# Feed-forward steps in three token phases of 12, 18 and 6 steps, with 30 of 36 steps in seven products

## The chip, the cores and the metric

One core of one Trainium2 chip runs the whole program. The metric is device time in microseconds (us): the median over three runs of the kernel before is 1127.13 us (1123.15 to 1127.32). The engines have short names in the profile: PE is TensorE (matmuls), PEld its weight loads, DVE is VectorE, ACT is ScalarE, POOL is GpSimd, SP is SyncE, which here issues nearly all DMA transfers (SPq is its queue). SBUF is the on-chip memory, PSUM the accumulators that the matmuls write.

## The reference

Both halves read the same tokens x (2048 tokens, 576 features); a gate mixes them.

```python
g = _sigmoid((x * gate_w).sum(-1, keepdims=True))
a = _A_ref(x, A_wqkv, A_wo)                  # linear attention, 32 heads of 18
y = _layernorm(x, axis=-1)                   # B: 576 -> 4608 -> 576
h = _gelu(jnp.einsum("bsd,df->bsf", y, w1) + b1)
b = jnp.einsum("bsf,fd->bsd", h, w2) + b2
return g * a + (1 - g) * b
```

All data is fp32. An fp32 matmul is made of several products of high and low parts ("fp32r" tiles): a value is split by a copy to fp32r on ACT (the high part) and a subtraction on DVE (the low part).

## The kernel before

**Stages.** Roughly the first 280 us compute the attention half and leave g times attention in DRAM (`late_acc`). The rest, which is all that the change touches, is the feed-forward half B. It is cut in two: the 2048 tokens into two super-blocks of 1024 (1 block is 2 x 512), the 4608 hidden features into 18 chunks of 256 (`NCHUNK`). One **step** is one chunk for one super-block, so there are 36 steps: steps 0 to 17 for super-block 0, steps 18 to 35 for super-block 1. Step 18 takes the chunk of step 17 again, whose weights are still in place (`HALF_TIME`, line 61).

**A step.** The *up* part multiplies the normalised tokens (tile `y`) by the chunk of w1 (tiles `wa` and `wb`) in the seven products of a Strassen-Winograd scheme (`FACTORS`, `UP_ORDER`; 7 matmuls of 512 columns each, so 49 in a step), and then GELU gives `h`. The *down* part multiplies `h` by the chunk of w2 (tile `region`) and adds the result to the accumulators (tile `accs`). It has two forms. In a **seven-product step** (`SEVEN`, line 64) there are 14 units of 6 matmuls of 288 columns: 84 matmuls. Four sums of parts of h must first be made (`make_sum`, line 1000; tile `u`), each then split, and four sums of w2 (`sum_w2`). In a **plain step** there are 8 units of 12 matmuls: 96, and no sums. Before, the seven-product steps are 1, 3, ... 15 and 17 to 34 (26 steps); plain are 0, 2, ... 16 and 35 (10 steps). The last step's units go to the output at once (`make_end`).

A down unit ends in an **eviction** (`evict`, line 1171): DVE adds PSUM to the accumulator, `accs<-ps,accs`, 12 in a seven-product step and 4 in a plain one. The other four of a plain step are seeded (`SEEDS`): ACT puts the old accumulator into PSUM first and copies the sum back. Two PSUM pairs take turns, so that a unit waits for the eviction two units before.

**Weights.** In steps 0 to 16 w1 of the next chunk is made from the input (`make_w1`, line 1025): SP loads it (8 transfers), POOL makes four sums of 384 columns (tile `fresh`), ACT and DVE split it into `wa` and `wb` (DVE: rows `wa<-fresh,wa` and `wb<-fresh,wb`), and SP stores the split parts in DRAM (`w1d`). In the second half these are only loaded back, one transfer for each of the seven factors (`load_split_w1`). w2 of a chunk is loaded and split in every step (`make_w2`; DVE rows `region<-fresh,region`).

**Tokens of super-block 1.** They are normalised, summed, split and stored to DRAM (`yd`) beside the first half (`make_y`, line 1204): DVE rows `accs<-accs` and `ystage<-...`. At the switch of super-blocks SP loads the seven parts of `y`, each as soon as the last product of step 17 that reads it is done; eight finishing operations on DVE (`make_finish`) mix the accumulators with attention and SP writes them out.

**The order of the work.** Every engine runs its instructions in the order in which the program lists them. A planner writes that order (`plan`, line 1278, and what follows): each operation has a cost in ns and a due time, and a list scheduler picks the next one for each engine. DVE has 9 `h` places, 5 `u` places and 7 `region` places to work with. Operations marked `port` (two inputs in SBUF) of DVE and POOL are kept apart in the plan; the program itself does not enforce that.

Of the kernel before, what the change touches and what calls it, by code (L numbers as in the profile page):

```python
# [60 lines left out]
LAST = 2 * NCHUNK - 1  # L61
SLOTS = 14
LAG = 3
# [8 lines left out]
FIRST_LANDS = 9000  # L72
SEEDS = ((0, 0, 0), (0, 1, 0), (1, 0, 0), (1, 1, 0))
SUM_ENGINE = {S1: "POOL", S3: "POOL", S2: "POOL", S4: "POOL"}
# [7 lines left out]

# [18 lines left out]
class InOrder:  # L101
# [5 lines left out]
    def __getattr__(self, name):  # L107
        op = getattr(self.engine, name)
        return lambda *args, **kwargs: self.tc.keep_in_program_order(op(*args, **kwargs))  # L109
# [3 lines left out]
def tile_gated_mix(ctx: ExitStack, tc: tile.TileContext, x, xm, xe, wm, we, wvm, wve, wo, um, ue, w2, b1, b2, gw, out):  # L113
# [670 lines left out]
    def chunk_of(k):  # L784
        return k if k < HALF_TIME else (k + NCHUNK - 1) % NCHUNK
# [72 lines left out]
    attn = [spare[:, n * D:(n + 1) * D] for n in range(6)] + [fresh[:, n * D:(n + 1) * D] for n in range(2)]  # L858
# [6 lines left out]
    class Op:  # L865

        def __init__(self, engine, f, ns, tail, needs, gives, port, take, give, by):
            self.engine, self.f, self.ns, self.tail = engine, f, ns, tail
            self.needs, self.gives, self.port = list(dict.fromkeys(needs)), gives, port
            self.take, self.give, self.by = take, give, by  # L870
            self.ready = 0.0

    ops, waiting, known, makers = [], {}, {}, {}
    rooms = {"h": [(0, n) for n in range(H_BUFS)], "u": [(0, n) for n in range(U_BUFS)],
             "w2": [(0, n) for n in range(W2_BUFS)]}
    lines = {name: [] for name in rooms}

    def op(engine, f, cols=0, needs=(), gives=(), port=False, take=None, give=(), ns=None, tail=None, more=0, by=None,
           early=0):
# [4 lines left out]
        o = Op(engine, f, ns, tail, needs, gives, port, take, give, by)  # L884
        o.early = early
# [7 lines left out]

    places = {}
    us = lambda key: u_places[:, places["u", key][0]]
    h_of = lambda key: h_places[:, places["h", key][0]]
    w2_key = lambda k, m: (k - (k == HALF_TIME), m)
    w2_of = lambda key: region[:, places["w2", w2_key(*key)][0]]
# [27 lines left out]
    def w1_key(k, a):  # L926
        return [("w1", k - (k == HALF_TIME), a)] if k else []
# [20 lines left out]
    def make_up(k):  # L948
        X, Yb, Z = [next(ff_banks) for _ in range(3)]
        free = lambda b: bank_users[b]  # L950
        y_in = lambda n: [("y", k // NCHUNK, FACTORS[n][1])] if k % NCHUNK == 0 else []
# [48 lines left out]
    def make_sum(k, m):  # L1000
# [4 lines left out]
        engine = SUM_ENGINE[m]  # L1005
# [16 lines left out]
    def dma(f, needs, gives, ns, service, early=0):  # L1022
        op(DMA, f, needs=needs, gives=gives, ns=ns, tail=service, early=early)
# [38 lines left out]
    def make_w2(k):  # L1062
        if k == HALF_TIME:
            return
# [449 lines left out]
```

## Time and profile before

| what | value |
|---|---|
| median of three runs | 1127.13 us |
| the profiled execution | 1125.78 us |
| its span (first to last instruction) | 1124.1 us |
| time outside the span | 1.7 us |
| granted TensorE clock | 1.00 |
| first up matmul of step 0 | 279.6 us from the span's start |

A "windows" view gives for each stretch of the span how long each engine was busy and, in brackets, how many instructions it had. A "lines" view groups instructions by line, engine and tiles and gives the mean duration of one, then the idle time of its engine just before. Nearly all instructions are recorded by one helper line (109), so the tiles name the work: `accs<-ps,accs` reads ps (PSUM) and accs and writes accs. A "waits" view says which engine waited for whom.

### The profile page before, as it was taken

To read this page: it belongs to the slowest core of one execution; us is meant where nothing else is said; L and a number is where in the kernel's file an instruction comes from. 1 tells how busy PE (TensorE), PEld (TensorE's weight loads), DVE (VectorE), ACT (ScalarE), POOL (GpSimd) and SP (SyncE) were. 2 spreads that over 40 slices of the span, in tenths; PEclk is the share of its full clock that TensorE was granted. 3 is DMA by queue.
4 is the path that set the end of the run, shared out by engine and by line. 5 is a ranking of instruction groups with operands and counts; after the bars stand their busy time and mean duration, and the time that the engine had idled before them with its cause. 6 is when DMAs were issued, how large, how long until landed. Compare 5 with 4: busy or idle time off the path is not lost.

```text
span 1124.1 us, 18584 instructions
## 1 busy us (share of the span) xinstructions
PE 1108.0 (99%) x6766; PEld 1003.5 (89%) x6766; DVE 888.7 (79%) x1369; ACT 642.6 (57%) x1153; POOL 385.9 (34%) x325
## 2 busy tenths in 40 slices
PE   9999999999999999999999999999999999999998
PEld 8999889999889888898988888888888888888888
DVE  4567685896787889979979997877887778778888
ACT  6667565453556665666756666345554555455542
POOL 2111112342334252634515453315433443344430
PEclk9999999999999999999999999999999999999999
DMA  6269853554636546473564549764445444444432
GB/s 177 64 88 286 168 171 141 225 204 160 210 122 213 187 162 213 150 267 126 186 221 154 197 166 373 280 234 129 120 123 147 127 115 127 138 127 124 120 109 85
DMA packets 109086, 189.42 MB, mean 169 GB/s; under 512 B 8892, under 2 KB 69068, under 8 KB 104898
## 3 DMA queue, kind: packets, MB, share of 16 engines
q1 hardware_dynamic: 108114, 187.49, 52.7%
q8 instruction: 53, 0.87, 0.3%
q10 hardware_dynamic: 720, 0.74, 0.2%
q14 instruction: 39, 0.32, 0.1%
q0 software_dynamic: 160, 0.01, 0.1%
HBM read 121.40 MB, written 66.80 MB: 167 GB/s over the span
## 4 chain that ended last, share of the span: by engine, by line
PE 72%; DVE 14%; ACT 4%; DMA 4%; issue 3%; POOL 2%; SPq 1%; ACTq 0%; DVEq 0%; POOLq 0%
PE ps L109 72%; DVE accs L109 3%; DVE h L109 3%; DMA fresh<-in_w 2%; DVE region L109 2%; SPq L109 1%; DVE wa L109 1%; POOL u L109 1%; DVE wb L109 1%; DVE den L109 1%; ACT h L109 1%; ACT u L109 1%; POOL fresh L109 1%; DVE u L109 1%; DMA w1d<-wb 0%
## 5 line engine op out<-in xcount | busy, mean ns | idle before, releaser
L109 PEld LDWEIGHTS ps<-region,h 128*128 128x128 f32 x3144 | 453.7, 188 | 45.9 <-DVE accs L109 10.0
L109 PE MATMUL ps<-region,h 128*128 128x288 f32 x3144 | 480.9, 296 | 4.0 <-DVE accs L109 2.0
L109 DVE TENSOR_TENSOR accs<-ps,accs 128x576 f32<-128x576 f32 x336 | 250.3, 752 | 89.8 <-PE ps L109 87.0
L109 POOL TENSOR_TENSOR fresh<-fresh 128x288 f32<-128x288 f32 (+1 forms) x164 | 173.8, 1066 | 406.2 <-DMA fresh<-in_w 332.0
L109 PE MATMUL ps<-y,wa 128*128 128x512 f32 x1008 | 269.7, 393 | 1.4 <-ACT ps L109 1.1
L109 PE MATMUL ps<-y,wb 128*128 128x512 f32 x756 | 204.3, 396 | 1.2 <-ACT u L109 1.0
L109 PEld LDWEIGHTS ps<-y,wa 128*128 128x128 f32 x1008 | 176.3, 188 | 27.2 <-DVE wa L109 1.7
L109 DVE TENSOR_TENSOR h<-u,h 128x512 fp32r<-128x512 f32 x222 | 177.1, 811 | 7.2 <-ACT u L109 4.3
L109 POOL TENSOR_TENSOR u<-u 128x512 f32<-128x512 f32 x104 | 152.3, 1465 | 88.1 <-DVE h L109 46.8
L109 PEld LDWEIGHTS ps<-y,wb 128*128 128x128 f32 x756 | 132.5, 188 | 24.7 <-ACT u L109 1.6
L109 PE MATMUL ps<-y 128*128 128x288 f32 (+1 forms) x896 | 126.9, 297 | 3.6 <-DVE acc L109 2.2
L109 ACT ACTIVATE u<-ps 128x512 f32<-128x512 f32 x73 | 43.7, 598 | 151.4 <-PE ps L109 151.4
L109 PEld LDWEIGHTS ps<-y 128*128 128x128 f32 x896 | 122.3, 188 | 7.0 <-DVE acc L109 3.4
L109 DVE TENSOR_TENSOR region<-fresh,region 128x576 fp32r<-128x576 f32 x120 | 107.8, 898 | 2.4 <-ACT region L109 1.9
L109 ACT ACTIVATE region<-fresh 128x576 fp32r<-128x576 f32 x120 | 73.9, 628 | 33.9 <-PE ps L109 33.9
L109 ACT ACTIVATE h<-ps,b1s 128x512 fp32r<-128x512 f32 x45 | 30.9, 687 | 81.9 <-PE ps L109 81.8
L109 ACT ACTIVATE h<-u,b1s 128x512 fp32r<-128x512 f32 x73 | 52.6, 721 | 32.7 <-DVE u L109 32.7
L109 ACT ACTIVATE h<-u 128x512 fp32r<-128x512 f32 x104 | 60.2, 622 | 12.4 <-POOL u L109 12.2
L109 PE MATMUL ps<-wp,qt 128*128 128x288 f32 x448 | 63.6, 298 | 1.2 <-DVE qt L109 1.2
L109 DVE TENSOR_TENSOR u<-ps,u 128x512 f32<-128x512 f32 x73 | 50.2, 688 | 15.7 <-ACT u L109 12.1
L109 DVE TENSOR_TENSOR wa<-fresh,wa 128x512 fp32r<-128x512 f32 x64 | 50.6, 791 | 14.8 <-ACT wa L109 13.9
L109 PEld LDWEIGHTS ps<-wp,qt 128*128 128x128 f32 x448 | 60.0, 188 | 1.7 <-DVE qt L109 1.7
(122 smaller groups left out, 994.9 us busy)
## 6 DMA issues: line engine op xcount, KB each, us to landing
w1d<-wa SPq DMA_DIRECT2D x17, 1280.0 KB
wa<-w1d SPq DMA_DIRECT2D x68, 320.0 KB
fresh<-in_w SPq DMA_DIRECT2D x70, 288.0 KB
y<-yd SPq DMA_DIRECT2D x14, 1280.0 KB
w1d<-wb SPq DMA_DIRECT2D x17, 960.0 KB
wb<-w1d SPq DMA_DIRECT2D x51, 320.0 KB
yd<-ystage SPq DMA_DIRECT2D x28, 320.0 KB
fresh<-in_um SPq DMA_DIRECT2D x64, 128.0 KB
```

The lines of the kernel that those rows point to most:

```text
L109: return lambda *args, **kwargs: self.tc.keep_in_program_order(op(*args, **kwargs))
```

## The change

1. **Three phases.** Steps 0 to 11 are chunks 0 to 11 for super-block 0; steps 12 to 29 all 18 chunks for super-block 1; steps 30 to 35 the last six chunks for super-block 0 again. At step 12 the accumulators of super-block 0 are mixed with attention and stored in `late_acc` (partial results); at step 30 super-block 1 is finished and written out, and super-block 0 starts again from zero (first evictions are ACT copies); at step 32 the partial results are loaded, and the end adds to them. Tokens change twice, so y is loaded twice (7 transfers of 1280 KB each time).
2. **Seven-product steps** are 30: 1, 4, 6, 7, and 9 to 34. Plain are 0, 2, 3, 5, 8 and 35. There are five seeds in a plain step instead of four.
3. **w1 of chunks 12 to 17** is made in the middle phase (`make_prep`), piece by piece through the two staging places of `ystage` (ACT copy, two DVE subtractions, one store, 7 pieces a chunk), and loaded back in steps 24 to 29 and 31 to 35. In the first phase `make_w1` is left for chunks 1 to 11.
4. **Sums of h**: S2, S3 and S4 are made by DVE (`u<-u` on DVE) instead of POOL; S1 stays on POOL.
5. **Super-block 1's tokens** must be ready by step 12 instead of step 18. Two attention places move from `fresh` to `ystage`.
6. **The planner** is new: a `port` operation is also held back in the plan if it would be in the way of an earlier due one of the other engine, DMA is planned with issue, transfer and at most 8 under way, each kind of operation has its own offset to its due time (`TUNED`), and a POOL operation is made to wait (a semaphore) for the `port` operation of DVE that the plan has ahead of it, if that ends less than 4 us before.

```diff
-SEVEN = {*range(1, NCHUNK - 1, 2), *range(NCHUNK - 1, LAST)}
-EARLY, LATE_, SLOP, SLACK = 0, 3, 30, 300
-Y_EARLY = 10000
-SEEDS = ((0, 0, 0), (0, 1, 0), (1, 0, 0), (1, 1, 0))
-SUM_ENGINE = {S1: "POOL", S3: "POOL", S2: "POOL", S4: "POOL"}
+SPLIT=12
+SWITCH = (SPLIT, SPLIT + NCHUNK)
+STEPS = [(0, c) for c in range(SPLIT)]
+STEPS += [(1, c) for c in (SPLIT - 1, *range(SPLIT - 1), *range(SPLIT, NCHUNK))]
+STEPS += [(0, c) for c in (NCHUNK - 1, *range(SPLIT, NCHUNK - 1))]
+PREP = [14, 15, 18, 21, 18, 27]
+DVE_SUMS = set([(2, False), (2, True), (4, False), (4, True), (6, False), (6, True)])
+SEEDS = ((0, 0, 0), (0, 0, 1), (0, 1, 0), (0, 1, 1), (1, 1, 1))
...
-        engine = SUM_ENGINE[m]
+        engine = DVE if (m, k < SPLIT) in DVE_SUMS else POOL
...
-        if seeded:
+        if seeded or first and k == SWITCH[1]:
             op(ACT, lambda: copy(to, pair_ap(p)), needs=needs, gives=[key], ns=543, tail=653)
...
+    def make_prep(c):
+        at = PREP_AT(c)
+        dma(lambda: load_w1(c), raw_free["w1"] + [("p", at, 1)], [("w1raw", c)], 3200, 8)
+        for n in range(4):
+            op(POOL, lambda n=n: sum_w1(c, (n,)), 384, needs=[[("w1raw", c)], [("w1sum", c, 0)], [("w1sum", c, 1)],
+                                                              [("w1raw", c), ("w1sum", c, 0)]][n],
+               gives=[("w1sum", c, n)], port=True)
+        raw_free["w1"] = []
+        for n, a in enumerate((A11, A12, A22, S1, S2, S4, S3)):
+            at = 7 * c + n
+            to, src = y_stage[:, at % 2:at % 2 + 1], wr(c)[:, a:a + 1]
...
+            op(ACT, lambda to=to, src=src: copy(to[:, :, 0:3], src), 3 * P, needs=needs + stage_free[at % 2],
+               gives=[("phi", at)])
+            op(DVE, low, 2 * P, needs=[("phi", at)], gives=[("plo", at)], port=True)
+            op(DVE, tail, P, needs=[("phi", at)], gives=[("ptl", at)], port=True)
+            dma(store, [("plo", at), ("ptl", at)], [("w1st", c, a)], 820, early=W_EARLY)
...
+    end, sequence = plan(*TUNED)
...
+        if o.port and o.engine == DVE:
+            before = dve.last.ins.name, t
+        if o.port and o.engine == POOL and before and before[1] > s - 4000:
+            tc.add_manual_dep(pool.last.ins, before[0], mybir.DependencyInfo(
+                mybir.DependencyClass.Sync, mybir.DependencyReason.DATA), reason="order")
```

Three places show how this moves instructions. The first is DVE in a steady run of seven-product steps; `accs<-ps,accs` are evictions, `h<-u,h` low parts of h, `u<-ps,u` a sum out of PSUM, `region` rows low parts of w2. Before (second half):

```order
L109 TENSOR_TENSOR accs<-ps,accs 128x2x288 x3
L109 TENSOR_TENSOR u<-ps,u 128x512
L109 TENSOR_TENSOR h<-u,h 128x512
L109 TENSOR_TENSOR accs<-ps,accs 128x2x288 x2
L109 TENSOR_TENSOR region<-fresh,region 128x2x288
L109 TENSOR_TENSOR accs<-ps,accs 128x2x288
L109 TENSOR_TENSOR u<-ps,u 128x512
L109 TENSOR_TENSOR accs<-ps,accs 128x2x288
L109 TENSOR_TENSOR h<-u,h 128x512
```

The same engine now, in the middle phase; `ystage<-fresh,ystage` are pieces of w1 for a later chunk and `u<-u` the sums of h:

```order
L117 TENSOR_TENSOR ystage<-fresh,ystage 64x128 x2
L117 TENSOR_TENSOR accs<-ps,accs 128x2x288 x2
L117 TENSOR_TENSOR u<-ps,u 128x512
L117 TENSOR_TENSOR h<-u,h 128x512
L117 TENSOR_TENSOR ystage<-fresh,ystage 128x256
L117 TENSOR_TENSOR accs<-ps,accs 128x2x288 x2
L117 TENSOR_TENSOR h<-u,h 128x512
L117 TENSOR_TENSOR u<-u 128x512
L117 TENSOR_TENSOR accs<-ps,accs 128x2x288
L117 TENSOR_TENSOR u<-u 128x512
L117 TENSOR_TENSOR u<-ps,u 128x512
L117 TENSOR_TENSOR accs<-ps,accs 128x2x288
```

Sums and pieces of w1 now stand between the evictions. The second place is POOL in the same stretch; `fresh<-fresh` of 288 columns are sums of w2, of 384 columns sums of w1. Before:

```order
L109 TENSOR_TENSOR u<-u 128x512 x4
L109 TENSOR_TENSOR fresh<-fresh 128x288 x4
L109 TENSOR_TENSOR u<-u 128x512 x4
L109 TENSOR_TENSOR fresh<-fresh 128x288 x4
L109 TENSOR_TENSOR u<-u 128x512 x4
```

And now:

```order
L117 TENSOR_TENSOR fresh<-fresh 128x288 x5
L117 TENSOR_TENSOR u<-u 128x512
L117 TENSOR_TENSOR fresh<-fresh 128x384 x4
L117 TENSOR_TENSOR fresh<-fresh 128x288 x2
L117 TENSOR_TENSOR u<-u 128x512
L117 TENSOR_TENSOR fresh<-fresh 128x288 x6
```

A run of four sums of h in a row has become one, and sums of w1 have come in. The third place is the queue of SP ahead of step 29, the last that loads prepared weights for super-block 1; `w1d_133` is the DRAM place of chunk 17, `w1d_132` of chunk 16. In the plan before the loads at the end of its second half stood like this:

```order
L109 DMA wa<-w1d_132 128x640 x3
L109 DMA fresh<-in_w 128x2x288 x2
L109 DMA wa<-w1d_132 128x640
L109 DMA wb<-w1d_132 128x640 x3
L109 DMA fresh<-in_w 128x2x288 x2
```

Now the stores of a chunk's pieces stand between the loads, for chunk 17 its own:

```order
L117 DMA w1d_133<-ystage 128x640
L117 DMA wb<-w1d_132 128x640 x3
L117 DMA wa<-w1d_133 128x640
L117 DMA w1d_133<-ystage 128x640
L117 DMA wa<-w1d_133 128x640
L117 DMA w1d_133<-ystage 128x640 x2
L117 DMA fresh<-in_w 128x2x288 x2
L117 DMA wa<-w1d_133 128x640 x2
L117 DMA w1d_133<-ystage 128x640
L117 DMA wb<-w1d_133 128x640
```

A store waits in SP's queue for DVE, and the loads behind it wait with it.

More of the change, by code (lines that the diff above doesn't have):

```diff
@@ L784, in chunk_of @@
     def chunk_of(k):
[L785 removed]
+        return STEPS[k][1]
     def w1_of(a):
@@ L883, in op @@
             tail = ns + c
-        o = Op(engine, f, ns, tail, needs, gives, port, take, give, by)
-        o.early = early
+        o = Op(engine, f, ns, tail, needs, gives, port, take, give, by, early, issues)
         ops.append(o)
@@ L1365, in tile_gated_mix @@
[L1365 to L1377 removed]
+    ups = [o for o in ops if o.engine == PE and o.by[0] == "up"]
+    downs = [o for o in ops if o.engine == PE and o.by[0] == "down"]
+    followers = {o: [u for key in o.gives for u in users.get(key, ())] for o in ops}
@@ L1470, in tile_gated_mix, with start @@
-    while any(pending.values()):
-        picks = [(x[0], n, x[1]) for n, e in enumerate((PE, ACT, DVE, POOL, DMA)) if (x := choose(e))]
-        assert picks, {e: [(o.by, o.gives, o.needs) for o in v][:3] for e, v in pending.items()}
-        s, _, o = min(picks, key=lambda x: x[:2])
-        commit(s, o)
-    assert not any(missing[o] for o in ops), [o.gives for o in ops if missing[o]][:5]
+        def start(o):
+            s = max(free[o.engine], ready[o])
+            if o.take:
+                name, keys = o.take
+                if line[name][at[name]] is not o or len(room[name]) < len(keys):
+                    return None
+                s = max(s, sorted(t for t, _ in room[name])[len(keys) - 1])
+            if o.port:
+                s = max(s, port_until[POOL] - 135 if o.engine == DVE else port_until[DVE] + 78)
+            return s
```

411 lines of the change are left out of this document (222 added, 189 removed).

## Prediction

> **What bounds the kernel now.** I read the engine totals first, then a table of stretches, then who waits for whom.
>
> ```profile
> PE 1108.0 (99%) x6766; PEld 1003.5 (89%) x6766; DVE 888.7 (79%) x1369; ACT 642.6 (57%) x1153; POOL 385.9 (34%) x325
> ```
>
> PE is busy almost always. Its busy time counts overlapping matmuls, though, so I work with the time from one stretch's start to the next's. In the table of stretches the columns are length, then busy time (instructions) of PE, PEld, DVE, ACT and POOL, the clock, the DMA share and GB/s. The edges are starts of steps: step 0; steps 1 to 17; 18 and 19; 20 to 33; 34; 35 with the end.
>
> ```profile
> 279.60:292.00 12.40, 11.40 (x51) 9.12 (x50) 4.28 (x7) 7.73 (x13) 1.02 (x1) 1.00 0.58 186
> 292.00:695.60 403.60, 399.30 (x2359) 355.21 (x2359) 351.48 (x500) 256.97 (x419) 168.38 (x133) 1.00 0.56 192
> 695.60:742.40 46.80, 45.70 (x268) 40.35 (x268) 37.76 (x52) 21.26 (x37) 15.73 (x12) 1.00 0.75 274
> 742.40:1060.30 317.90, 317.85 (x1864) 283.69 (x1863) 249.69 (x351) 168.05 (x280) 128.34 (x112) 1.00 0.48 135
> 1060.30:1083.30 23.00, 22.89 (x135) 20.27 (x134) 18.40 (x26) 12.01 (x20) 8.84 (x8) 1.00 0.44 126
> 1083.30:1124.10 40.80, 37.40 (x243) 34.51 (x241) 34.27 (x50) 14.01 (x23) 2.60 (x2) 0.99 0.24 82
> ...
> 1107.08 13.75 PE L109 MATMUL ps<-region,h 128*128 128x288 f32 x102
> ```
>
> The last row is from the order of instructions in time: 102 down matmuls of the end without a gap. Less 0.3 us for the length of the last one, 13.45 / 101 = **0.133 us** is the price of a down matmul. Steps 20 to 33 take 317.9 / 14 = **22.7 us** each, with 49 up and 84 down matmuls, so an up matmul costs (22.7 - 84 x 0.133) / 49 = 0.235 us. At these prices the whole feed-forward part, 1764 up and 3144 down matmuls, is 415 + 418 = 833 us; 3.3 us lie between the last matmul's start (1120.8) and the end. It takes 1124.1 - 279.6 = 844.5 us. So about **8 us** are lost against the clean rate: 0.9 in step 0, 4.8 in steps 1 to 17 (833 x 0.235 + 1524 x 0.133 = 398.8 of 403.6), 1.4 in steps 18 and 19, 0.8 at the end. PE's own work is the bound; what else can be won is those 8 us.
>
> Two rows of waits for steps 1 to 17 say what the 4.8 us are:
>
> ```profile
> PEld ps L109 <- ACT ps L109: 6.8, 14, 1.1
> PEld ps L109 <- DVE accs L109: 5.1, 7, 1.1
> ```
>
> Weight loads wait for a PSUM pair that an eviction on DVE, or a copy on ACT, has not left yet. Two seven-product stretches show the cause:
>
> ```profile
> 408.90:433.40 24.50, 23.37 (x136) 20.11 (x135) 23.96 (x31) 15.30 (x25) 12.07 (x9) 1.00 0.37 128
> 505.00:528.90 23.90, 23.05 (x134) 20.16 (x133) 23.32 (x32) 15.00 (x25) 12.36 (x9) 1.00 0.36 122
> ```
>
> DVE is busy 23.96 of 24.5 us and 23.32 of 23.9, and these stretches are 1.8 and 1.2 us longer than a clean 22.7. At 249.69 / 317.9 = 79% DVE, steps 20 to 33 lose nothing.
>
> **The change, part by part.** *Four more seven-product steps.* Each has 84 down matmuls in place of 96: 4 x 12 x 0.133 = **-6.4 us**, on PE, which sets the end. If every loss went as well, the span would be 279.6 + 833 - 6.4 + 3.3 = 1109.5 us, and the time, with the 1.7 us outside the span, **1111.2 us**. The rest is how much is lost anew; call it e, today 8.
>
> *The middle phase.* A clean seven-product step has 249.69 / 14 = 17.8 us of DVE, and POOL 128.34 / 14 = 9.2. Now come three sums of h and 14 small subtractions for each of six chunks.
>
> ```profile
> L109 DVE TENSOR_TENSOR h<-u,h x222: 671/681/1776, 292.9 to 1110.5; 128x512 fp32r<-128x512 f32 x111
> L109 DVE TENSOR_TENSOR ystage<-accs,ystage x28: 410/418/426, 346.8 to 686.3; 128x256 fp32r<-128x256 f32 x28
> L109 DVE SCALAR_TENSOR_TENSOR ystage<-ystage,low_rows,accs x28: 339/345/349, 347.8 to 686.6; 128x128 fp32r<-128x128 f32 x28
> L109 POOL TENSOR_TENSOR u<-u x104: 1287/1304/1882, 310.9 to 1087.0; 128x512 f32<-128x512 f32 x104
> ```
>
> These rows give shortest, median and longest duration in ns. No sum of h has run on DVE. The nearest row is `h<-u,h`, as large and with both inputs in SBUF: 0.68 us, between 0.67 and 1.78; I take the median, since the order now keeps POOL away from it. Three make 2.0 us. A piece of w1 costs 0.42 + 0.35 us, the nearest rows for its two subtractions, so 42 pieces over 18 steps are 1.8 us a step. DVE comes to **21.6 of 22.7 us, 95%**. POOL loses three sums of 1.3 us and takes 24 sums of w1 over 18 steps; it has room and I cost that at nothing.
>
> *The first phase.* Steps 1 to 11 must carry all the work on super-block 1's tokens. Its DVE rows, and those of w1, for the first half of the feed-forward part (busy us, mean ns; behind the bar the idle time before them):
>
> ```profile
> L109 DVE TENSOR_TENSOR h<-u,h 128x512 fp32r<-128x512 f32 x94 | 82.9, 897 | 6.0 <-ACT u L109 4.3 <-ACT h L109 1.5
> L109 DVE TENSOR_TENSOR region<-fresh,region 128x576 fp32r<-128x576 f32 x43 | 44.0, 1024 | 2.3 <-ACT region L109 1.9
> L109 DVE TENSOR_TENSOR wa<-fresh,wa 128x512 fp32r<-128x512 f32 x32 | 32.6, 1019 | 13.9 <-ACT wa L109 13.9
> ...
> L109 DVE TENSOR_TENSOR wa<-fresh,wa 64x256 fp32r<-64x256 f32 x32 | 18.0, 563 | 0.9
> L109 DVE TENSOR_TENSOR accs<-accs 128x768 f32<-128x768 f32 x16 | 16.1, 1009 | 0.0
> L109 DVE TENSOR_TENSOR wb<-fresh,wb 128x768 fp32r<-128x768 f32 x16 | 15.3, 958 | 0.1
> L109 DVE TENSOR_TENSOR ystage<-accs,ystage 128x256 fp32r<-128x256 f32 x28 | 11.7, 417 | 4.0 <-ACT ystage L109 4.0
> L109 DVE SCALAR_TENSOR_TENSOR ystage<-ystage,low_rows,accs 128x128 fp32r<-128x128 f32 x28 | 9.6, 344 | 0.0
> L109 DVE TENSOR_TENSOR accs<-accs 128x384 f32<-128x384 f32 x16 | 9.2, 574 | 0.3
> L109 DVE TENSOR_TENSOR wb<-fresh,wb 64x384 fp32r<-64x384 f32 x16 | 8.9, 556 | 0.5
> ```
>
> Tokens: 16.1 + 9.2 + 11.7 + 9.6 = 46.6 us. w1: 32.6 + 18.0 + 15.3 + 8.9 = 74.8 us for 16 chunks, 4.7 each. Before, steps 1 to 17 hold about eight seven-product down parts (8 x 17.8 = 142), nine plain ones, all of that w1 and the tokens, in 351.5 us of DVE: a plain part is left with (351.5 - 142 - 74.8 - 46.6) / 9 = 9.8 us, now 9.0 (one eviction of 0.75 goes to ACT). Steps 1 to 11 of the new order carry six seven-product down parts with three sums (6 x 19.8), five plain (5 x 9.0), ten chunks (47) and the tokens: 119 + 45 + 47 + 46.6 = **258 us**. Their clean length is 11 x 22.7 + 5 x 12 x 0.133 = **258 us**. Before it was 351.5 of 398.8, 88%. So at today's durations DVE would be full.
>
> Today's durations hold time in which POOL blocks DVE: `h<-u,h` takes 897 ns here against a median of 681 in the whole run. I estimate unblocked durations of 0.75 us for `region` and 0.68 and 0.42 for the two rows of `wa`, as `h` has them for the same number of columns. Blocked are then 94 x 0.216 + 43 x 0.274 + 32 x 0.34 + 32 x 0.14 = 47 us behind 133 POOL instructions, **x = 0.36 us for each**; in steps 20 to 33 `h` runs at 736 ns and `region` at 1037, which makes 98 x 0.055 + 42 x 0.287 = 17 us behind 112, x = 0.16. These are the two rows:
>
> ```profile
> L109 DVE TENSOR_TENSOR h<-u,h 128x512 fp32r<-128x512 f32 x98 | 71.1, 736 | 0.0
> L109 DVE TENSOR_TENSOR region<-fresh,region 128x576 fp32r<-128x576 f32 x42 | 43.6, 1037 | 0.0
> ```
>
> The new order puts a POOL instruction behind a DVE one, where evictions follow, and evictions are not blocked (752 ns in steps 20 to 33, 750 in the first half). I halve x for the first phase: 70 POOL instructions x 0.18 = 12 us less, 246 of 258 us, 95%. The added wait stands on POOL; queued behind it are POOL's other sums, and ACT's copies into `region` and `h` wait for those. POOL was busy only 168 of 403.6 us here, so I cost the wait itself at nothing; it would cost a late sum if DVE ran late.
>
> How much 95% loses lies between 0 (steps 20 to 33, at 79%) and 1.5 us a step (the two stretches at 98%), over 24 seven-product steps: e between 0 and 36. I take the middle of the first phase's rows there, 0.5 us for its six seven-product steps, because tokens and w1 come in lumps, and 0.1 us for the 18 even steps of the middle: 3 + 2 us.
>
> *The switches.* Step 18 moves 396 GB/s and is still clean; step 19 loses 1.4.
>
> ```profile
> 695.60:718.30 22.70, 22.70 (x135) 20.21 (x135) 18.64 (x26) 10.38 (x19) 6.99 (x7) 1.00 1.01 396
> 718.30:742.40 24.10, 23.00 (x136) 20.14 (x135) 19.12 (x27) 10.88 (x18) 8.74 (x6) 1.00 0.51 158
> PEld ps L109 <- ACT ps L109: 2.5, 4, 1.5
> ```
>
> The wait (third row, steps 17 to 20) is for ACT, which stands behind POOL's four sums in a row; with one left, 0.4 us at each of two switches. Eight more finishing operations of DVE fall where eight evictions of step 30 go to ACT. Step 0 and the end keep their 0.9 and 0.8. The stores of w1 pieces in SP's queue cost nothing as long as a load has its 22.7 us until the next step; for chunk 17 that slack is short, at most the 14.6 us that SP has waited for a staging piece, at least nothing, and nothing is what I take:
>
> ```profile
> SPq L109 <- DVE ystage L109: 22.5, 9, 14.6
> ```
>
> The sum: e = 3 + 2 + 0.8 + 1.7 = 7.5, rounded to 7. **1111.2 + 7 = 1118.2 us**, against 1125.8 for the profiled execution, which is 1.3 us under the median of the three runs; I leave that difference alone.
>
> **Rule against row.** The long `region` rows (750 ns median, 1.0 us mean) show blocking by POOL. The Trainium skill, page "SBUF — State Buffer", section "Who interferes with whom", says that a DVE instruction with two SBUF inputs and a GpSimd instruction that reads SBUF take one shared port exclusively, and that the loser blocks fully; by that rule x could reach the whole length of a POOL instruction. That the longest `h<-u,h` took 1776 ns agrees with it; the means of 0.16 and 0.36 us do not reach it. The third rival below is what this would do here.
>
> **The rivals.** *All losses go* (e from 0 to 3): 1113 us. For it: steps 20 to 33. Against: DVE at 95% has no such stretch before. Chance 0.17. *The forecast*, e from 3 to 11: 0.45. *DVE becomes the bound in the even steps too*: 0.6 us on 24 seven-product steps, e about 17, so 1128 us, no change, and the saved matmuls are paid back in evictions. For it: 408.9 to 433.4. Against: that stretch has four POOL sums of h in a row. Chance 0.20. *POOL blocks DVE longer*: without blocking, a middle step has 21.6 - 17 / 14 = 20.4 us of DVE and 6.3 POOL instructions (5 + 24 / 18), so DVE needs more than 22.7 us once x passes 0.37 us. At x = 0.5 the middle loses 18 x 0.85 = 15 us and the first phase, 258 - 70 x 0.36 + 70 x 0.5 = 268, loses 10: e = 27 with the rest, **1138 us**, slower. For it: x was 0.36 where DVE was fullest. Against: fewer and shorter POOL instructions, and an order made for it. Chance 0.18.
>
> **How the numbers follow.** About 0.5%, 5.6 us, is what a measurement of this kernel can tell from no change. Faster by more needs e under 9: the first case and most of the second, 0.17 + 0.37 = 0.54. Within 0.5%: the rest of the second and the third, 0.28. Slower: 0.18. The range of 1111 to 1136 leaves out a few in a hundred below and about 0.15 above.
>
> **What would show it.** 48 down matmuls fewer (3096) at 0.133 us; middle steps of 22.7 to 22.9 us with DVE busy near 95%; `h<-u,h` under 750 ns in the first phase; the loss of the first phase in waits of weight loads for `accs`. The forecast is wrong if middle steps take over 23.3 us, if POOL's sums come late behind their new waits, or if a product waits for a transfer at steps 12, 29 or 30.

## The result, and the profile after

The changed kernel takes **1134.14 us** (median of 4 runs, 1133.26 to 1135.96), the kernel before 1125.89 beside it: ratio 1.0078, 95% interval 1.0053 to 1.0104. It is 0.8% slower where 0.7% faster was forecast: inside the stated range of 1111 to 1136 us, but at its slow end and on the other side of no change. The profiled execution took 1133.88 us, its span is 1132.2.

The engine totals of the changed kernel, then its table of stretches, cut at the starts of steps 0, 1, 12, 30 and 35 and at the end:

```profile
PE 1104.8 (98%) x6718; PEld 996.9 (88%) x6718; DVE 934.9 (83%) x1551; ACT 643.4 (57%) x1185; POOL 266.1 (24%) x263
```

```profile
280.00:292.10 12.10, 11.41 (x51) 9.14 (x50) 4.77 (x8) 6.51 (x11) 0.76 (x1) 1.00 0.63 212
292.10:559.90 267.80, 257.79 (x1513) 228.12 (x1512) 240.25 (x377) 173.96 (x285) 74.32 (x73) 1.00 0.63 220
559.90:977.30 417.40, 411.53 (x2397) 364.23 (x2396) 370.11 (x592) 225.06 (x399) 108.07 (x112) 1.00 0.63 195
977.30:1091.20 113.90, 113.86 (x668) 101.43 (x667) 92.51 (x138) 61.81 (x105) 21.25 (x22) 1.00 0.58 181
1091.20:1132.20 41.00, 37.44 (x242) 34.42 (x241) 34.85 (x52) 13.61 (x23) 0.00 (x0) 0.99 0.24 81
```

PE has 48 matmuls fewer (6718 for 6766). The second row holds 539 up matmuls (11 steps of 49) and, of its 1513, 974 down. At the prediction's prices, 0.235 and 0.133 us, that is 256.2 us of 267.8: 11.6 lost. The third holds 882 and 1515: 208.8 of 417.4, that is 408.8, 8.7 lost with the prices unrounded. I call these numbers **the loss** of a stretch, and work them out in the same way for every kernel, good to about 0.2 us. A plain step comes out 0.5 us below its price, so a stretch with plain steps can have a negative loss.

| loss in us | step 0 | steps 1-11 | steps 12-29 | steps 30-34 | end |
|---|---|---|---|---|---|
| before | 0.9 | 2.8 | 3.4 | 0.3 | 0.4 |
| forecast | 0.9 | 3 | 2 and 0.8 for switches | 0 | 0.8 |
| after | 0.6 | 11.6 | 8.7 | 0.3 | 0.6 |

So the matmuls were saved, and about 14 us more were lost. The losses are not spread: in the first phase step 5 alone loses 5.2 and step 4 2.7; in the middle, steps 17, 18, 19, 22 and 24 lose 2.0, 1.3, 1.1, 1.8 and 1.1, and the others little. The four steps at the two switches (12, 13, 30, 31) lose 0.3 us at most.

Who waits for whom says where to look. The rows are of the changed kernel, the first phase (first fence) and the middle (second): engine and tile, what it waited for, us in total, times, longest (`yd<-ystage` are stores of token pieces, `w1d<-ystage` of pieces of w1).

```profile
ACT wa L117 <- POOL fresh L117: 14.6, 8, 2.8
...
ACT ystage L117 <- DMA yd<-ystage: 9.3, 7, 4.2
PEld ps L117 <- ACT ps L117: 8.4, 8, 3.7
PEld ps L117 <- DVE accs L117: 7.2, 12, 1.2
```

```profile
ACT ystage L117 <- DMA w1d<-ystage: 16.5, 7, 3.0
...
PEld ps L117 <- DVE accs L117: 9.2, 20, 1.3
PEld ps L117 <- DVE region L117: 3.3, 4, 1.1
```

Besides the late evictions that were foreseen ACT now has two waits that were hardly there before: for stores of staged pieces (before, once, for 3.8 us) and, in the first phase, for POOL's sums of w1 (before, in the same steps, 0.5 us). PE in turn waits for ACT. The order in time inside step 5 shows how a wait for a store becomes a wait of PE (start, duration, what it is, and in square brackets the idle time before it):

```profile
391.82 0.35 SPq L117 DMA_DIRECT2D yd<-ystage  x1
...
396.86 0.52 ACT L117 ACTIVATE ystage<-accs 128x384 fp32r<-128x384 f32 x1 [1.99 <-DMA yd<-ystage]
397.29 0.63 ACT L117 ACTIVATE accs<-ps 128x576 f32<-128x576 f32 x1
397.82 0.67 ACT L117 ACTIVATE region<-fresh 128x576 fp32r<-128x576 f32 x1
398.40 0.62 ACT L117 ACTIVATE h<-u 128x512 fp32r<-128x512 f32 x1
398.92 0.64 ACT L117 ACTIVATE ps<-ps 128x576 f32<-128x576 f32 x1
...
399.61 1.86 PE L117 MATMUL ps<-region,h 128*128 128x288 f32 x12 [3.33 <-ACT ps L117]
```

The store is issued at 391.82, and the copy that reuses its staging place starts 5.0 us later. ACT takes its work in the listed order: the eviction of a seeded unit (`accs<-ps`), two splits (`region`, `h`) and the next seed (`ps<-ps`) stand behind that copy, and PE idles 3.33 us for the seed.

A stretch of step 19 in the middle shows the other engine. POOL makes two sums of w1:

```profile
727.05 2.45 POOL L117 TENSOR_TENSOR fresh<-fresh 128x384 f32<-128x384 f32 x2 [6.06 <-DMA wb<-w1d]
727.27 1.35 DVE L117 TENSOR_TENSOR u<-u 128x512 f32<-128x512 f32 x1
...
728.54 2.11 DVE L117 TENSOR_TENSOR h<-u,h 128x512 fp32r<-128x512 f32 x2
...
731.37 0.80 PE L117 MATMUL ps<-region,h 128*128 128x288 f32 x4 [0.82 <-DVE region L117]
```

Beside those 2.45 us of POOL, DVE's sum takes 1.35 us in place of the middle's mean of 0.71, and its two low parts 2.11 in place of 1.48 (twice 0.742); what they delay, PE waits for.

### The profile page after: what moved, and what is told of

Same layout as the page of the kernel before. It is cut to its first block, busy times and chain, and to the rows that moved or that the text cites. A ratio compares the mean times of both kernels' runs of the same rounds, so it can differ in the third digit from the quotient of the medians.

```text
span 1132.2 us, 18790 instructions
## 1 busy us (share of the span) xinstructions
PE 1104.8 (98%) x6718; PEld 996.9 (88%) x6718; DVE 934.9 (83%) x1551; ACT 643.4 (57%) x1185; POOL 266.1 (24%) x263
## 4 chain that ended last, share of the span: by engine, by line
PE 62%; DVE 20%; DMA 7%; ACT 4%; issue 3%; SPq 2%; POOL 1%; ACTq 0%; DVEq 0%; POOLq 0%
PE ps L117 62%; DVE accs L117 6%; DVE h L117 4%; DVE u L117 3%; DVE region L117 3%; SPq L117 2%; DMA yd<-ystage 2%; DVE ystage L117 1%; DMA fresh<-in_ue 1%; POOL fresh L117 1%; DVE wa L117 1%; DVE wb L117 1%; DMA w1d<-ystage 1%; ACT u L117 1%; DMA fresh<-in_um 1%
## 5 line engine op out<-in xcount | busy, mean ns | idle before, releaser
L117 PEld LDWEIGHTS ps<-region,h 128*128 128x128 f32 x3096 | 446.8, 188 | 59.3 <-DVE accs L117 18.1
L117 DVE TENSOR_TENSOR accs<-ps,accs 128x576 f32<-128x576 f32 x356 | 263.3, 751 | 34.2 <-PE ps L117 32.2
L117 POOL TENSOR_TENSOR fresh<-fresh 128x288 f32<-128x288 f32 (+1 forms) x176 | 165.9, 946 | 514.5 <-DMA fresh<-in_w 169.2
L117 DVE TENSOR_TENSOR h<-u,h 128x512 fp32r<-128x512 f32 x234 | 165.8, 732 | 12.2 <-ACT u L117 11.8
L117 DVE TENSOR_TENSOR region<-fresh,region 128x576 fp32r<-128x576 f32 x124 | 87.5, 715 | 2.0 <-ACT region L117 1.5
L117 DVE TENSOR_TENSOR u<-u 128x512 f32<-128x512 f32 x90 | 65.9, 733 | 7.8 <-POOL u L117 7.4
L117 ACT ACTIVATE h<-u 128x512 fp32r<-128x512 f32 x120 | 71.0, 618 | 2.0 <-DVE u L117 2.0
L117 ACT ACTIVATE h<-ps,b1s 128x512 fp32r<-128x512 f32 x41 | 28.1, 685 | 64.3 <-PE ps L117 64.2
L117 POOL TENSOR_TENSOR u<-u 128x512 f32<-128x512 f32 x30 | 38.8, 1294 | 101.7 <-DVE h L117 81.7
```

Source lines behind the costliest of these rows:

```text
L117: self.last = self.tc.keep_in_program_order(op(*args, **kwargs))
```

## The experiments

All ratios stand against the kernel before on the same chip. Differences in us between two kernels go across chips, on which the kernel before took 1124.5 to 1125.9 us, so they are good to about 1 us; the losses come from one profiled execution each. The kernels that leave work out keep the changed kernel's planned order, unless it says otherwise.

| kernel | us | ratio to before, 95% interval | loss in steps 1-11 | 12-29 |
|---|---|---|---|---|
| changed kernel | 1134.14 | 1.0078, 1.0053 to 1.0104 | 11.6 | 8.7 |
| no staging stores | 1125.02 | 0.9999, 0.9986 to 1.0012 | 5.6 | 6.2 |
| no subtractions of pieces | 1126.24 | 1.0017, 1.0004 to 1.0029 | 6.7 | 4.7 |
| no waits on POOL | 1150.25 | 1.0223, 1.0183 to 1.0263 | 14.3 | 19.3 |
| all sums of h on POOL | 1150.66 | 1.0232, 1.0203 to 1.026 | 29.6 | 7.8 |
| no w1 pieces | 1123.3 | 0.999, 0.998 to 1.0 | 12.2 | -2.2 |
| no sums of w1 in the middle | 1129.38 | 1.0046, 1.003 to 1.0062 | 11.5 | 3.3 |
| longer stores in the plan | 1133.13 | 1.0081, 1.0066 to 1.0096 | 12.5 | 8.2 |
| two phases, 26 seven-product steps | 1121.67 | 0.9976, 0.9965 to 0.9986 | 6.3 | -2.3 |
| two phases, 30 | 1123.26 | 0.9983, 0.9971 to 0.9996 | 7.4 | 4.0 |
| two phases, 30, tokens spread | 1133.04 | 1.0067, 1.0045 to 1.0089 | 7.5 | 12.2 |
| no tokens | 1120.1 | 0.9953, 0.9938 to 0.9969 | -3.0 | 8.2 |
| two phases, 26, sums on POOL | 1133.86 | 1.0074, 1.005 to 1.0098 | 16.8 | 0.5 |

### Which work the losses come from

**Tokens left out.** The loads, sums, splits and stores of super-block 1's tokens go; it reads those of super-block 0.

```diff
-dma(lambda j=j: load_pair(1, j), raw_free["rows"], [("yraw", j)], 2000, 7)
+dma(lambda j=j: None, raw_free["rows"], [("yraw", j)], 2000, 7)
...
-op(DVE, lambda j=j, n=n: sum_pair(1, j, n), 3 * P, port=True,
+op(DVE, lambda j=j, n=n: None, 3 * P, port=True,
```

> The changed kernel in its planned order, but the normalised tokens of super-block 1 are not made (their loads, sums, splits and stores are left out), and super-block 1 reads the tokens of super-block 0 instead. Theory A, tokens are what the first phase loses by: steps 1 to 11 lose at most 2 us (11.6 before), about 1124 us. Theory B, w1 and the three sums of h on DVE crowd it by themselves: 5 us or more stay in steps 1 to 11, 1128 us or longer. The middle phase keeps its 8.7 us in both.

The first phase of that kernel, in the columns of the table of stretches:

```profile
291.20:544.40 253.20, 253.20 (x1513) 229.30 (x1511) 192.86 (x289) 163.21 (x257) 70.75 (x73) 1.00 0.51 179
```

PE is busy for all 253.2 us. The loss is -3.0, the floor for a stretch with plain steps, and the kernel is 14.0 us faster. DVE went from 240.25 of 267.8 us (90%) to 192.86 of 253.2 (76%). Theory A holds: w1 of ten chunks and three sums of h on DVE are carried without loss, and tokens are what it loses by, 11.6 + 3.0 = 14.6 us. ACT's wait for POOL's sums of w1 goes with them, from 14.6 to 2.3 us.

**Pieces of w1 left out.** Loads, sums, splits and stores of chunks 12 to 17 go; the steps read chunks made in the first phase.

```diff
-op(POOL, lambda n=n: sum_w1(c, (n,)), 384, ...
+op(POOL, lambda n=n: None, 384, ...
...
-dma(store, [("plo", at), ("ptl", at)], [("w1st", c, a)], 820, early=W_EARLY)
+dma(lambda: None, [("plo", at), ("ptl", at)], [("w1st", c, a)], 820, early=W_EARLY)
```

> Leaves out all the making of w1 in the middle phase (loads, POOL sums, ACT copies, DVE subtractions, stores); chunks 12 to 17 read the weights of chunks 0 to 5; all other instructions keep their order. Today steps 12 to 29 lose 8.7 us. Theory D (the pieces of w1 are what the middle loses by): 1.5 us or less left there, about 1126 us. Theory E (the sums of h on DVE lose by themselves): 4 us or more left. Steps 1 to 11 should stay at 11 to 12 us under both.

**POOL's sums left out alone.** Here only the POOL sums of chunks 13 to 17 go, and the pieces are split from unsummed data.

```diff
-op(POOL, lambda n=n: sum_w1(c, (n,)), 384, ...
+op(POOL, lambda n=n: sum_w1(c, (n,)) if c == SPLIT else None, 384, ...
```

> Leaves out POOL's four sums of w1 in the middle phase for chunks 13 to 17, nothing else (the weights of those chunks are wrong). Theory C (these sums of 384 columns block DVE's low parts and make the w2 and h parts late): the middle loses 5 us or less instead of 8.7. Theory A (staging stores) or B (DVE is full by its own work): 7.5 us or more.

The middle phase without any pieces, and then with pieces but without POOL's sums:

```profile
559.60:966.10 406.50, 406.50 (x2396) 365.45 (x2395) 333.85 (x507) 208.26 (x357) 83.05 (x88) 1.00 0.51 154
```

```profile
559.30:971.20 411.90, 409.56 (x2395) 364.43 (x2395) 363.83 (x591) 224.59 (x399) 87.36 (x91) 1.00 0.64 197
```

Without pieces PE is busy throughout, and the middle is 10.9 us shorter. Half of that, 417.4 - 411.9 = 5.5 us, comes back when POOL alone is relieved: its busy time falls by 20.7 us and DVE's by 6.3, though DVE has the same 591 or 592 instructions. That is 0.31 us of DVE for each of the 20 sums left out. Theories D and C hold: the work that I had costed at nothing, because POOL has room, lengthens DVE's work, and weight loads then wait for DVE: 5.6 us for evictions in place of 9.2, and no longer at all for low parts of w2 (3.3). That POOL, busy with w1, is late with its sum of h is the smaller part: DVE waits 2.7 us for it in place of 4.9. The losses by step say the same. In the changed kernel steps 17, 19, 22 and 24, each with three or four of these sums, lose 2.0, 1.1, 1.8 and 1.1 us; without the sums 0.8, -0.3, -0.1 and -0.3. Step 14, where the sums of chunk 12 stay, keeps its 0.7 or 0.8. Step 27 has four sums and loses nothing with them either, so the price depends on what they meet.

**Stores left out.** Neither tokens nor pieces are stored; the loads read what is there already (tokens of super-block 0, chunks 0 to 11).

```diff
-dma(lambda j=j, part=part: store_pair(1, j, part), [("ylo", at), ("ytl", at)], [("yst", at)], 820, early=Y_EARLY)
+dma(lambda: None, [("ylo", at), ("ytl", at)], [("yst", at)], 820, early=Y_EARLY)
...
-dma(store, [("plo", at), ("ptl", at)], [("w1st", c, a)], 820, early=W_EARLY)
+dma(lambda: None, [("plo", at), ("ptl", at)], [("w1st", c, a)], 820, early=W_EARLY)
```

> Leaves out the stores of all staging pieces (super-block 1's tokens and w1 of chunks 12 to 17); super-block 1 then reads super-block 0's tokens, and chunks 12 to 17 the weights of chunks 0 to 5. Order, ACT and DVE work stay. Today steps 1 to 11 lose about 11.6 us and steps 12 to 29 about 8.8 us against the clean rate. Theory A (ACT's copies wait for the store that frees one of two staging places, and ACT's later work waits behind them): first phase down to about 6, middle to 3 or less, about 1123 us. Theory B (DVE is full): within 3 us of the changed kernel, 1131 to 1135 us.

**Subtractions left out.** DVE's low parts of tokens (all but those of the first two pieces) and of pieces go. A POOL instruction that waited for one of them now waits for the DVE instruction ahead of it, so this takes away two things.

```diff
-op(DVE, low, 2 * P, needs=[("phi", at)], gives=[("plo", at)], port=True)
-op(DVE, tail, P, needs=[("phi", at)], gives=[("ptl", at)], port=True)
+op(DVE, lambda: None, 2 * P, needs=[("phi", at)], gives=[("plo", at)], port=True)
+op(DVE, lambda: None, P, needs=[("phi", at)], gives=[("ptl", at)], port=True)
```

> Leaves out the DVE subtractions of the staging pieces (all but the first two pieces of tokens): about 20 us of DVE less in the first phase and 30 us less in the middle; stores and ACT copies stay. Theory B (DVE is full): first phase loses 4 us or less instead of 11.6, middle 2 instead of 8.8, about 1120 us. Theory A (staging stores): ACT still waits for stores, middle still loses 5 us or more, 1127 us or more.

**More time for stores in the plan.** Stores are planned at 5.0 us in place of 3.0, so that the planner puts the next copy later; nothing is left out.

```diff
-dma(store, [("plo", at), ("ptl", at)], [("w1st", c, a)], 820, early=W_EARLY)
+dma(store, [("plo", at), ("ptl", at)], [("w1st", c, a)], 2800, early=W_EARLY)
```

> The plan takes 5.0 us instead of 3.0 for a store of a staging piece, as the trace shows between such a store's issue and the ACT copy that it releases (4 to 5 us); all else as changed. Theory A (ACT waits at a copy that the plan thought free): the plan puts other ACT work ahead of it, steps 1 to 11 lose about 8 instead of 11.6 and 12 to 29 about 6.5 instead of 8.7, 1128 us. If the places themselves are too few, a later copy moves the loss to the tokens or to DVE: 1132 us or more.

Leaving stores out brings 6.0 us in the first phase, as theory A said, and 2.5 in the middle, where it had asked for nearly 6; 1125.0 us is far from theory B's 1131. Leaving subtractions out brings 4.9 and 4.0, less than theory B asked, and the middle falls below theory A's 5 us: neither is the whole. Telling the planner of the longer store took away ACT's wait for stores, 25.8 us in 14 waits of the changed kernel (9.3 in the first phase, 16.5 in the middle) and 0.2 us now, and yet the losses stayed: 12.5 and 8.2, in other steps, as the second case of the expectation had it. The order is a new one there, so this alone does not tell what the wait is worth. But without POOL's sums of w1 the order was kept, ACT's wait for stores in the middle stayed at 17.5 us, and the loss there fell to 3.3. So ACT's wait at the staging place, which the order in time shows so plainly, does not measure the loss. What the stores cost beside that wait (their place in SP's queue, their transfers, or copies that come too late for the next piece) stays open.

### The waits of POOL, and who makes the sums

**Without the waits.** The three lines that make a POOL instruction wait for DVE go; the order on each engine is the same.

```diff
-        if o.port and o.engine == POOL and before and before[1] > s - 4000:
-            tc.add_manual_dep(pool.last.ins, before[0], mybir.DependencyInfo(
-                mybir.DependencyClass.Sync, mybir.DependencyReason.DATA), reason="order")
```

> The planned order without the added semaphore waits of POOL on DVE. Theory W (these waits make POOL's sums late): POOL idle for DVE goes, 2 to 6 us faster, 1128 to 1132 us. Theory P (they protect DVE, whose low parts of h now take 732 ns against 811 before): low parts of h rise to 780 ns or more and the time to 1136 us or more. Theories A and B alone: no change.

It is 16.1 us slower, so in this order the waits are worth that much. Theory P's time came, but not its sign: low parts of h in the first half take 720 ns without the waits and 711 with them. Other rows lengthened, in the middle phase (changed kernel, then without waits; behind the bar busy us and mean ns):

```profile
L117 DVE TENSOR_TENSOR u<-u 128x512 f32<-128x512 f32 x54 | 38.5, 712 | 5.2 <-POOL u L117 4.9
...
L117 DVE TENSOR_TENSOR ystage<-fresh,ystage 64x128 fp32r<-64x128 f32 x42 | 12.6, 313 | 1.0
...
L117 POOL TENSOR_TENSOR fresh<-fresh 128x384 f32<-128x384 f32 x24 | 25.5, 1069 | 52.1 <-DMA wa<-w1d 14.2 <-DMA wb<-w1d 12.1 <-DVE accs L117 12.1
```

```profile
L117 DVE TENSOR_TENSOR u<-u 128x512 f32<-128x512 f32 x54 | 42.0, 777 | 6.0 <-POOL u L117 5.9
...
L117 DVE TENSOR_TENSOR ystage<-fresh,ystage 64x128 fp32r<-64x128 f32 x42 | 15.6, 386 | 1.0
...
L117 POOL TENSOR_TENSOR fresh<-fresh 128x384 f32<-128x384 f32 x24 | 28.9, 1222 | 39.6 <-DMA fresh<-in_ue 22.5 <-DMA wa<-w1d 10.6 <-DMA w1d<-ystage 6.1
```

DVE's busy time in the middle goes from 370.11 to 379.27 us with the same work, and the loss from 8.7 to 19.3. That agrees with blocking in both directions, as the Trainium skill has it (page "SBUF — State Buffer", section "Who interferes with whom"); it is spread over many rows, on DVE by less than a tenth of a microsecond each and on POOL's sums of w1 by 0.15.

**All four sums of h on POOL**, in the changed kernel, planned anew:

```diff
-DVE_SUMS = set([(2, False), (2, True), (4, False), (4, True), (6, False), (6, True)])
+DVE_SUMS = set()
```

> S2, S3 and S4 back on POOL, planned anew, all else as changed: 90 instructions of 0.68 us less on DVE, 90 of 1.3 us more on POOL. Theory B (DVE is full) with blocking of 0.2 us for each POOL instruction: about 40 us of DVE less over 30 steps, loss halved, about 1124 us. Theory A (staging stores): within 4 us of the changed kernel. A third theory, that POOL's row of sums and its blocking of DVE are worse than the sums themselves: 1140 us or more.

It is 16.5 us slower, as the third theory had it: step 8 alone loses 14.3 and step 11 6.4. With this planner, whose offsets were left as they were, moving sums to DVE was no mistake, however full DVE is.

### Without the third phase

**Two phases.** Super-block 0 for 18 steps, then super-block 1; no partial results, no pieces, the 26 seven-product steps of the kernel before. The new planner, the waits and the sums on DVE stay.

```diff
-SPLIT=12
-SWITCH = (SPLIT, SPLIT + NCHUNK)
+SPLIT = NCHUNK
+SWITCH = (SPLIT,)
...
+SEVEN = {*range(1, NCHUNK - 1, 2), *range(NCHUNK - 1, LAST)}
```

> The two super-blocks of 18 steps and the 26 seven-product steps of before, with all the rest of the change (new plan and its offsets, sums on DVE, waits of POOL, five seeds). Its clean time is 6.4 us above that of the change, 1117.6 us. Theory F (what loses is the crowding of the first phase and the w1 pieces; planner and DVE sums are sound): 4 to 6 us lost, 1122 to 1124 us. Theory G (planner, waits and DVE sums lose by themselves): 10 us or more lost, 1128 us or more.

It loses 4.9 us in all, so theory F holds. At 1121.67 us it is the fastest full version found, 0.24% under the kernel before. That lies inside the 0.5% that I called measurable at the start; with the runs made here the interval excludes 1.

**The same with all sums on POOL** (`DVE_SUMS = set()`):

> The kernel of two phases with 26 seven-product steps that took 1121.7 us, with all four sums of h on POOL as in the kernel before, planned anew. Theory A, the sums on DVE are what makes that kernel 2.7 us faster than before: with them back on POOL it takes 1124.5 us or longer. Theory B, the planner and the waits of POOL make it, whichever engine has the sums: within 1 us of 1121.7.

Theory A: 1133.86 us, 12.2 more. It is also slower than the kernel before, whose sums are on POOL without waits. So with this planner the waits go with sums on DVE. A new plan with sums on POOL and without the waits was not run, nor were the planner's offsets set anew, so the plan stays a possible cause beside the waits. These waits in steps 1 to 11, of the kernel before and of this one, speak for the waits of POOL:

```profile
ACT h L109 <- POOL u L109: 5.1, 4, 1.6
PEld ps L109 <- ACT ps L109: 3.9, 8, 1.0
POOL u L109 <- DVE h L109: 3.5, 3, 2.1
```

```profile
POOL u L116 <- DVE region L116: 12.9, 6, 4.4
PEld ps L116 <- ACT ps L116: 9.1, 6, 4.5
ACT h L116 <- POOL u L116: 7.1, 8, 2.5
```

With the waits a sum on POOL stands behind low parts of w2 on DVE (12.9 us, no such row before), ACT waits for the sum, and PE for ACT. DVE is only 85% busy there (232.99 of 274.6 us) and the loss is 16.8. A part of that is the clock: the granted TensorE clock is 0.57 on average in 323 to 327, 425.5 to 429.5 and 473 to 481 us.

**Two phases with 30 seven-product steps.**

```diff
-SEVEN = {*range(1, NCHUNK - 1, 2), *range(NCHUNK - 1, LAST)}
+SEVEN = {1, 3, 5, 7, *range(9, LAST)}
```

> Two super-blocks of 18 steps, as in the kernel before (no partial results, no w1 pieces in a middle phase), with the changed kernel's planner, sums and waits, and now 30 seven-product steps (1, 3, 5, 7 and 9 to 34) in place of the 26 of the kernel with two phases that took 1121.7 us. Theory A, losses come only where tokens and w1 are made: four more seven-product steps save 6.4 us; steps 9 to 17 carry w1 of eight chunks but few tokens, so steps 1 to 11 lose 6 to 8 us and steps 12 to 29 at most 2: 1115 to 1119 us, faster than before (1124.5). Theory B, each seven-product step beside the making of w1 crowds DVE by as much as it saves PE: the losses of steps 1 to 17 grow by 5 us or more, 1121 us or longer.

The steps that become seven-product steps are 10, 12, 14 and 16, and a down part is multiplied during the next step. So three of the four fall into steps 12 to 17, which are these rows, with 26 and then with 30 seven-product steps:

```profile
554.50:693.80 139.30, 139.30 (x837) 126.32 (x836) 101.17 (x151) 90.49 (x146) 33.64 (x35) 1.00 0.51 178
```

```profile
554.60:694.70 140.10, 138.35 (x801) 120.38 (x800) 136.00 (x207) 84.26 (x135) 48.92 (x52) 1.00 0.57 202
```

36 matmuls fewer and 0.8 us more. The three plain steps gave DVE its air (101.2 of 139.3 us), and without them it is busy 136.0 of 140.1 us, 97%, as long as PE's clean time of 136.2. Weight loads wait 7.4 us for its evictions there, and not once with 26. DVE sets the pace. Theory B holds: steps 1 to 17 lose 6.8 us more (11.3 for 4.5), for 6.4 saved.

**The tokens spread** over steps 0 to 16, with plain steps 2, 5, 8 and 11 between them:

```diff
-SEVEN = {1, 3, 5, 7, *range(9, LAST)}
+SEVEN = {1, 3, 4, 6, 7, 9, 10, 12, 13, *range(14, LAST)}
...
-dma(lambda j=j: load_pair(1, j), raw_free["rows"], [("yraw", j)], 2000, 7)
+dma(lambda j=j: load_pair(1, j), raw_free["rows"] + ([("p", 4 * j, 1)] if j else []), [("yraw", j)], 2000, 7)
```

> As the kernel of two phases with 30 seven-product steps, but these are 1, 3, 4, 6, 7, 9, 10, 12 to 34, and the tokens of super-block 1 are spread: pair j of them is not loaded before the first product of step 4j. Theory A, the first phase loses because tokens of one super-block crowd into its first eleven steps: spread over sixteen, no step loses over 1 us and steps 1 to 17 lose under 5 us in all, about 1114 us. Theory B, the work on DVE in steps 1 to 17 is what counts, wherever it stands: they lose 7 us or more, 1118 us or longer.

Theory A falls and theory B's time comes: steps 1 to 17 lose 20 us. But where the work stands does matter. Steps 1 to 11 lose 7.5 us, as before the spreading (7.4), and the last pair of tokens now meets seven-product steps at 12 and 13, which lose 5.7 and 3.0. Spreading moved the work of tokens in among seven-product steps that have none to spare.

## Why the prediction was wrong

**Right.** PE bounds the kernel, and each matmul saved is worth 0.133 us: with tokens left out steps 1 to 11 run without loss, with pieces left out the middle does. The switches cost nothing that can be seen (0.8 forecast), and no product waits for a transfer there. Nor was DVE's work misjudged: 240.25 us in the first phase (246 forecast) and 370.11 / 18 = 20.6 a middle step (21.6 forecast). These rows of the first phase bear on blocking:

```profile
L117 DVE TENSOR_TENSOR h<-u,h 128x512 fp32r<-128x512 f32 x64 | 44.1, 711 | 2.2 <-ACT u L117 1.9
L117 DVE TENSOR_TENSOR region<-fresh,region 128x576 fp32r<-128x576 f32 x26 | 22.1, 852 | 1.6 <-ACT region L117 1.5
L117 DVE TENSOR_TENSOR wa<-fresh,wa 128x512 fp32r<-128x512 f32 x20 | 18.0, 899 | 5.9 <-ACT wa L117 5.6
L117 DVE TENSOR_TENSOR u<-u 128x512 f32<-128x512 f32 x19 | 15.9, 835 | 1.1 <-POOL u L117 1.0
...
L117 DVE TENSOR_TENSOR wa<-fresh,wa 64x256 fp32r<-64x256 f32 x20 | 10.6, 532 | 0.5
```

Low parts of h take 711 ns, under the 750 that I had named as a sign. Against the unblocked durations that the prediction estimated (0.68, 0.75, 0.68, 0.68 for the sum, and 0.42) the rows hold 64 x 0.03 + 26 x 0.1 + 20 x 0.22 + 19 x 0.155 + 20 x 0.11 = 14 us behind 73 POOL instructions, 0.19 us each, and I had halved 0.36 to 0.18. The last rival ("POOL blocks DVE longer", 1138 us), in which that number rises to 0.5, is out: the time came within 4 us of its 1138, but not by its mechanism.

**Wrong: the step from DVE's share to the loss.** The prediction read what 95% busy costs from two stretches of the kernel before and took "0.5 us for its six seven-product steps" of the first phase "and 0.1 us for the 18 even steps of the middle: 3 + 2 us". They lost 11.6 and 8.7, and middle steps took 23.2 us on average instead of the 22.7 to 22.9 named as a sign. So e, all that is lost against the clean rate, was 21.8 us (0.6 + 11.6 + 8.7 + 0.3 + 0.6) instead of 7. The kernel before already spoke against 0.5 at 95%: the prediction's 4.8 us in eight seven-product steps, at 88%, are 0.6 each. DVE's share was not the reason. A share falls as a stretch grows longer, so it is best taken of the clean time: 240.25 of 256.2 us is 94% in the first phase and 370.11 of 408.8 is 91% in the middle, 95% forecast for both. Share and loss do not go together from kernel to kernel, in steps 1 to 11: at the same 94% the two phases with 30 seven-product steps lose 7.4 us (DVE 241.26 us) and the changed kernel 11.6, and the two phases with 26 lose 6.3 at 92% with sums on DVE (236.3 of 257.8 us) and 16.8 at 90% with sums on POOL. I read this so, without a run that isolates it: what is lost depends on which engine stands behind which at a given unit, and tokens and pieces add such links. Nor were the steps even: in the first phase steps 4 and 5 lose 7.9 of the 11.6 us, in the middle the loss sits mostly in steps with POOL's sums of w1.

**Wrong: two costs taken as nothing.** The stores of w1 pieces, bounded by 14.6 us and taken as "at least nothing, and nothing is what I take", go with 2.5 us of the middle's loss; the stores of tokens, for which the sum had no term, go with 6.0 of the first phase's (no stores). POOL's 24 sums of w1, "it has room and I cost that at nothing", go with 5.4 of the middle's 8.7 when 20 of them are left out. POOL did have room, at 26% busy in the middle; the price was on DVE. I had an x of 0.16 to 0.36 us per POOL instruction in hand and did not apply it to the 24 that the change adds to the middle; at 0.16 that is 4 us of DVE, beside a DVE 90% full; the 20 that were left out measured 0.31 each.

**The account.** Tokens cost the first phase 14.6 us and pieces the middle 10.9 (each alone left out). Taken off together, which was not run, 1134.1 - 14.0 - 10.8 = 1109.3 us would be left, near the clean 1111.2. Nothing large is left unexplained by stage; within a stage the parts overlap (6.0 and 4.9 of 14.6 for stores and subtractions), and the rest of the tokens' price was not taken apart. One part of it may be ACT's 14.6 us of waiting for POOL's sums of w1. The prediction named late sums of POOL "behind their new waits" as a sign against it, and late they are; but without those waits ACT still waits 12.3 us, so it is not chiefly the waits that make them late, and what it costs PE is not shown.

**The rival of DVE as the bound**, with the saved matmuls paid back in evictions, 1128 us, is nearest in mechanism, and the two-phase kernels with 26 and 30 seven-product steps show it on its own. For the changed kernel it names only a part of the cause.

## What to carry to other kernels

A saved matmul pays only in a step in which the engines that feed PE have air. Before making a step shorter, work out what must be done inside it on each in-order queue, by step and not by phase, and give every instruction added to an idle engine the price that it has on its neighbour. An engine's busy share is no price list: the same 94% of the clean time went with 7.4 us lost in one order and 11.6 in another. And a wait that is plain in the trace may be only where the shortage surfaces; see whether the loss goes with it before believing it. Here the loss of the middle fell from 8.7 to 3.3 us while ACT's plain wait stayed.

## What the runs showed of the hardware

**The clock can halve after a pause of PE.** Behind the changed kernel's pause of 3.33 us at 399.61 the granted clock stays at 1.00 (read in steps of 2 us from 397 to 405). The kernel with spread tokens has a pause of 3.33 us too, ended by ACT, and behind it (stretches, then the matmuls in the order in time):

```profile
576.00:580.00 4.00, 4.00 (x15) 3.47 (x15) 3.60 (x6) 3.43 (x6) 2.72 (x3) 0.59 0.43 161
580.00:590.00 10.00, 10.00 (x58) 8.91 (x57) 9.63 (x18) 6.94 (x13) 3.47 (x4) 0.99 0.40 164
```

```profile
575.80 2.62 PE L116 MATMUL ps<-y,wb 128*128 128x512 f32 x7 [3.33 <-ACT u L116]
```

Seven up matmuls take 2.62 us in place of 1.77, and the clock is 0.50 for some 3.4 us. In the changed kernel with all sums on POOL it stayed down far longer, while PE paused again and again (2.97, 3.31 and 3.19 us):

```profile
474.00:488.00 14.00, 7.11 (x28) 6.41 (x29) 10.58 (x19) 4.80 (x9) 6.12 (x6) 0.52 0.44 144
```

So a pause can be paid for twice, and part of what that kernel lost at step 8 is clock. The Trainium skill (page "TensorE: Matmul & The Clock Gate", section "Part 1: The HAM clock gate") has the half clock follow an idle window of about 3.4 us and last until a busy one. The lengths agree. That the changed kernel's 3.33 us at 399.61 was not followed by it, and the other's was, fits windows that run on their own, which no row here shows directly. But a pause of 3.4 us is not needed: without POOL's waits the clock fell just before 860 us, where the longest pause was 1.74 us.

```profile
856.00:860.00 4.00, 1.67 (x10) 1.06 (x8) 4.00 (x5) 0.59 (x1) 2.69 (x2) 0.96 0.13 51
860.00:863.00 3.00, 3.00 (x10) 2.71 (x11) 2.36 (x4) 0.00 (x1) 0.00 (x0) 0.50 0.42 109
```

**A store's place comes free late.** From the issue of a staging store to the copy that waits for its place, 5.0 us passed at 391.82, where the plan of the changed kernel reckons with 3.0. Over the 14 such waits of the changed kernel it was 2.2 to 5.3 us.
